# Products x @ w_ch made in earlier chunks, two of them kept in the places of results, in an attention and spectral-mixing kernel

## Chip, cores, metric

One core of a Trainium2 chip. The metric is the time of the whole program on the device in microseconds, the median of several runs.

## The reference, cut to what matters

```python
x = attention(q, k, v, s)                    # 8 batches, 8 heads, 576 positions, 64 wide -> [8, 576, 512]
X = rfft(x, axis=1)[:, :64]                  # 64 modes
Y = X @ (w_r + i w_i)                        # one 512 x 512 complex matrix per mode: 134 MB of fp32 weights
y = irfft(Y, n=576)
u = x + y
out = u + max(u @ w_ch, 0)
```

By linearity u @ w_ch = x @ w_ch + y @ w_ch, so the part x @ w_ch, here called a *product*, can be made for each pair of 128-row blocks (18 pairs) before y is known.

## The kernel before

The mode weights come in 128 tiles of 512 KB (they are bf16 on the chip, half the size of the fp32 in memory) through one transfer queue and are used in four groups of eight *chunks*, four tiles a chunk. The last group's chunks run after the attention; between them TensorE makes products of *late* pairs, whose results are kept on chip. The product of a pair is 8 matmuls of 128x512, after 8 small ones that transpose x.

```python
    NLOC = 4
    places = [finpool.tile([P, 4 * DM], BF16, name=f"z1_{i}") for i in range(NLOC)]
    places.append(old[:, 4 * DM : 8 * DM])
    places += [y_acc[:, c : c + 2, :]... for c in (0, 2)]
    # later products: a buffer of the weight ring
    ...
    late = [i for i in kept if i not in first_pairs]
    TAKE = (2, 2, 1, 2, 0, 3)                # products in chunks 0 to 5 (one is made a step later)
    ...
    for c in range(NCK - 2):                 # chunks 0 to 5
        yb = modes(NG - 1, c)
        for x in range(TAKE[c] - 1):
            work()                           # transposes one late pair; makes the product of the one before
        yt = y_transposed(yb)
        if TAKE[c]:
            work()
        y_times_wch(c, yt)                   # v = y @ w_ch of this chunk
    work()
    c = NCK - 2                              # chunk 6
    for i in range(NPRE):                    # pairs 0 and 1 are not kept: their products stay in PSUM
        x_transposed(i)
    yb = modes(NG - 1, c)
    yt = y_transposed(yb)
    y_times_wch(c, yt)
    for i in range(NPRE):
        x_times_wch(i, False)
    start_u(0)                               # u 0 = x + ...
    add_y(us[0], 0, 0, slice(0, GK))         # ... + y of chunks 0 to 6; waits for the spread of y
    def first_sums():
        for i in range(NPRE):
            add_y(z_of(i), i, 1, slice(0, GK))   # waits for the spread of v
    yb = modes(NG - 1, NCK - 1, first_sums)  # chunk 7: three groups, first_sums, the last group
    # from here on, the tail: y and v of chunk 7, then sums, ReLU and output of 18 pairs
```

y and v of each chunk are *spread* by a transfer of 128 KB from one on-chip tile to another before the sums can use them.

The softmax here doesn't subtract the row's maximum and nothing guards it: scores larger than these inputs give would overflow.

## Time and profile before

| | before |
|---|---|
| time, median of 3 | 463.88 us (462.47 to 464.22) |
| span of the profiled execution | 462.2 us |
| TensorE busy, VectorE, ScalarE | 75%, 51%, 47% of the span |
| last weight tile lands | 421.6 us |
| last group of chunk 7 starts | 423.75 us |
| from there to the end | 38.45 us |

The span runs from the first to the last instruction of one profiled execution; the times are some 1.8 us above it. No engine's share says what bounds this kernel: one must look at the point where the weights end. The prediction shows those lines.

### The profile page before, as it was taken

Reading aid. Unit: us, or ns where it says so; the run is one execution under the profiler, and the core shown is the slowest. Engines: PE = TensorE matmul, PEld = TensorE weight load, DVE = VectorE, ACT = ScalarE, POOL = GpSimd, SP = SyncE. Lnnn points to the kernel's source line nnn. Section 1 sums busy time; section 2 is a strip of 40 time slices with the busy share of each in tenths; the row PEclk is TensorE's granted clock in tenths of the full one; section 3 lists DMA queues with packets and bytes.
Section 4 is the critical chain, followed back from the end, with each engine's and each line's share of the span. In section 5 each row is a group of like instructions: output and inputs, shape, how many; then the busy total and the mean of one; then the engine's idle time right before and its main releaser. Section 6 shows DMA issues by size and latency. Waiting matters only on the chain.

```text
span 462.2 us, 10263 instructions
## 1 busy us (share of the span) xinstructions
PE 345.9 (75%) x4185; PEld 215.8 (47%) x4185; DVE 233.6 (51%) x523; ACT 219.1 (47%) x382; POOL 182.9 (40%) x269
## 2 busy tenths in 40 slices
PE   1879968977663989647397586798976767578996
PEld 1556646755441666434265354565642423244442
DVE  7676654753332657524265335557553432171676
ACT  1677865564342667624265434556610202031895
POOL 6655544544444455344454444455232222100000
PEclk9998996995776899958789859899997767599999
DMA  9999999999999999999999999999999999992697
GB/s 179 201 202 203 202 200 203 203 204 204 204 204 198 204 202 203 204 204 205 199 194 205 204 204 205 205 202 202 206 211 213 215 212 214 214 210 59 223 307 302
DMA packets 110063, 95.16 MB, mean 206 GB/s; under 512 B 28544, under 2 KB 105216, under 8 KB 110016
## 3 DMA queue, kind: packets, MB, share of 16 engines
q0 software_dynamic: 98960, 81.81, 111.7%
q1 hardware_dynamic: 11056, 12.70, 8.9%
q8 instruction: 33, 0.54, 0.4%
q14 instruction: 14, 0.11, 0.1%
HBM read 164.66 MB, written 9.44 MB: 377 GB/s over the span
## 4 chain that ended last, share of the span: by engine, by line
DMA 66%; PE 22%; issue 4%; DVE 4%; POOL 3%; ACT 0%; DVEq 0%; POOLq 0%; ACTq 0%
DMA w_sb<-in_moe_w_i_dram 40%; DMA w_sb<-in_moe_w_r_dram 8%; DMA q<-in_q_dram 7%; DMA k<-in_k_dram 5%; PE yp L441 3%; PE av_ps L394 2%; PE sc_ps L365 2%; DMA x_all<-in_moe_w_r_dram 2%; PE z_ps L598 2%; DMA y_acc<-in_moe_w_r_dram 2%; PE z_ps L657 2%; DMA y_acc<-in_moe_w_i_dram 2%; PE u_ps L676 2%; PE tr_ps L324 2%; PE u_ps L657 2%
## 5 line engine op out<-in xcount | busy, mean ns | idle before, releaser
L373 ACT ACTIVATE p_sb<-sc_ps,cumt_sb 128x576 f16<-128x576 f32 (+1 forms) x256 | 141.8, 635 | 48.1 <-PE sc_ps L365 47.6
L217 POOL DMA_DIRECT2D w_sb<-in_moe_w_i_dram x60 | 45.0, 751 | 80.8 <-DMA w_sb<-in_moe_w_i_dram 34.1
L217 POOL DMA_DIRECT2D w_sb<-in_moe_w_r_dram x60 | 45.3, 756 | 69.4 <-DMA w_sb<-in_moe_w_r_dram 24.0
L217 POOL DMA_DIRECT2D v<-in_v_dram x72 | 50.7, 707 | 31.7 <-DMA v<-in_v_dram 9.5
L441 PE MATMUL yp<-w_sb,xs 128*32 128x512 bf16 x480 | 38.9, 424 | 24.9 <-DMA w_sb<-in_moe_w_i_dram 20.9
L324 PE MATMUL tr_ps<-ident,q 64*64 64x64 bf16 x576 | 17.2, 209 | 52.4 <-DMA q<-in_q_dram 52.4
L359 PE MATMUL sc_ps<-negm,ident 128*128 128x256 bf16 x256 | 56.0, 305 | 0.2
L327 DVE COPY qtA<-tr_ps 64x576 bf16<-64x576 bf16 x32 | 23.8, 743 | 46.8 <-PE tr_ps L324 46.8
L394 PE MATMUL av_ps<-v,p_sb 128*128 128x65 f16 x1024 | 45.8, 200 | 0.0
L344 ACT ACTIVATE p<-sc_ps,cumt 128x64 f16<-128x64 f32 x32 | 10.0, 313 | 72.0 <-PE sc_ps L340 72.0
L394 PEld LDWEIGHTS <-p_sb 128*128 128x128 f16 x1024 | 40.7, 102 | 5.1 <-issue 1.0
L365 PE MATMUL sc_ps<-qtB,ktB 128*128 128x512 bf16 (+2 forms) x192 | 42.3, 336 | 0.0
L327 DVE COPY ktA<-tr_ps 64x576 bf16<-64x576 bf16 x32 | 24.0, 749 | 33.3 <-PE tr_ps L324 33.2
L441 PEld LDWEIGHTS <-xs 128*32 128x32 bf16 x512 | 22.7, 169 | 36.3 <-issue 32.9
L324 PEld LDWEIGHTS <-q 64*64 64x64 bf16 x576 | 13.4, 121 | 55.2 <-DMA q<-in_q_dram 54.4
L365 PE MATMUL sc_ps<-qtA,ktA 65*128 65x512 bf16 (+2 forms) x192 | 38.2, 310 | 0.5 <-DMA qtA<-ncum_sb 0.5
L399 DVE TENSOR_REDUCE den<-av_ps 128x5 f32<-128x10 f32 x64 | 10.8, 169 | 51.1 <-PE av_ps L394 51.1
L404 DVE TENSOR_TENSOR x_all<-av_ps,rcp 128x320 f16<-128x320 f32 x64 | 31.4, 491 | 2.2
L327 ACT COPY ktB<-tr_ps 64x576 bf16<-64x576 bf16 x32 | 20.3, 633 | 21.4 <-DVE ktA L327 20.4
L324 PE MATMUL tr_ps<-ident,k 64*64 64x64 bf16 x576 | 17.2, 208 | 16.2 <-DVE qtB L327 10.3
L365 PEld LDWEIGHTS <-ktB 128*128 128x128 bf16 x192 | 21.8, 114 | 14.0 <-issue 5.2
L598 PE MATMUL z_ps<-wch_sb,xs 128*128 128x512 f16 x96 | 28.1, 448 | 0.0
(103 smaller groups left out, 516.4 us busy)
## 6 DMA issues: line engine op xcount, KB each, us to landing
w_sb<-in_moe_w_r_dram POOLq DMA_DIRECT2D x60, 512.0 KB, 11.9
w_sb<-in_moe_w_i_dram POOLq DMA_DIRECT2D x60, 512.0 KB, 11.9
q<-in_q_dram POOLq DMA_DIRECT2D x32, 144.0 KB, 9.8
k<-in_k_dram POOLq DMA_DIRECT2D x32, 144.0 KB, 10.1
v<-in_v_dram POOLq DMA_DIRECT2D x72, 64.0 KB, 9.7
out_dram<-r_sb SPq DMA_DIRECT2D x16, 256.0 KB, 2.1
out_dram<-r_w SPq DMA_DIRECT2D x16, 256.0 KB, 2.6
x_all<-in_moe_w_i_dram POOLq DMA_DIRECT2D x3, 512.0 KB, 9.8
```

The costliest lines, as they stand in the source:

```text
L217: nc.gpsimd.dma_start(out=dst, in_=src)
L324: nc.tensor.transpose(ps[rows, r, :], src[rows, r, :], ident16[rows, rows])
L327: copy(out=dst[n % NQ][rows, :].rearrange("d (p r) -> d p r", r=R), in_=ps[rows].rearrange("d r p -> d p r"),)
L359: nc.tensor.matmul(ps[:, bass.ds(w * S, W)], ident16, negm[:, bass.ts(r, W)], start=True, stop=False, skip_group_check=True,)
L365: nc.tensor.matmul(ps[:, c0 : c0 + i1 - i0], keys[:, w, r, :], qt[:, i0:i1], start=False, stop=True, skip_group_check=True,)
L373: nc.scalar.activation(out=pt[:, poff[x] : poff[x] + S - w * W], in_=ps[:, w * S : (w + 1) * S - w * W], func=ACTF.Exp, bias=cumt_sb[:, x, ...
L394: nc.tensor.matmul(ps[:, I, r : r + NCH], lhsT, rhs, start=(i == 0), stop=(i == len(todo) - 1), skip_group_check=True,)
L399: nc.vector.tensor_reduce(out=den, in_=ps[:, :, 0 : VW : NCH], axis=mybir.AxisListType.X, op=ALU.add)
L404: nc.vector.tensor_tensor(out=x_all[:, g, b, :, D * h : D * h + D], in0=ps[:, :, 1 : NCH], in1=rcp.unsqueeze(2).to_broadcast([P, NT, D]), ...
L441: nc.tensor.matmul(ps[32 * cg : 32 * cg + 32, :], cols[:, c0 : c0 + 32, c * MC + 2 * cg + par], wt[(g, c, ri, par)][:, cg, :], start=(x == ...
L598: nc.tensor.matmul(z[:, x, :], xts[i][:, x, dt, :], wch_sb[:, dt, :], start=(dt == 0), stop=(last and dt == DT - 1), skip_group_check=True,)
L657: nc.tensor.matmul(dst[x][r, :], G_sb[rows, bass.ds(T * P, r.stop - r.start)], yv[rows, bb, which, :], start=start, stop=True, skip_group_ ...
```

## The change

Its intent is to have no product left over when the last weights arrive. It finds three more places for kept products (two are the places where results 2 and 4 will be written, which needs pairs 2 and 4 to be the first late ones, so pair 9 takes pair 2's turn in the attention loop), moves the late products to chunks 0 to 4 (the last of them, made one step later, falls between chunks 5 and 6), and makes pair 0's product ahead of chunk 6.

```diff
-    first_pairs = [i for i in kept if pairs[i][0][1] < NF and pairs[i][0][0] <= 3]
+    first_pairs = [i for i in kept[1:] if pairs[i][0][1] < NF and pairs[i][0][0] <= 4][:6]
...
-    NLOC = 4
+    NLOC = 5
...
-    places = [finpool.tile([P, 4 * DM], BF16, name=f"z1_{i}") for i in range(NLOC)]
+    places = [finpool.tile([P, 4 * DM], BF16, name="r_sb", tag="r", bufs=3) for i in range(2)]
+    places += [finpool.tile([P, 4 * DM], BF16, name=f"z1_{i}") for i in range(NLOC)]
...
-    TAKE = (2, 2, 1, 2, 0, 3)
+    TAKE = (3, 2, 2, 2, 1, 0)
...
+    x_times_wch(0, False)
     yb = modes(NG - 1, c)
     yt = y_transposed(yb)
     y_times_wch(c, yt)
-    for i in range(NPRE):
-        x_times_wch(i, False)
+    x_times_wch(1, False)
```

(The results' tile is also declared in another type, of the same size.)

## The prediction

> **What bounds the kernel now.** I read the page first, then the chain of waits in order of time, then TensorE's timeline near its end. The page's row of DMA shares says that the transfers are full for 36 of 40 slices, and the row of bytes says what ends there:
>
> ```profile
> DMA  9999999999999999999999999999999999992697
> GB/s 179 201 202 203 202 200 203 203 204 204 204 204 198 204 202 203 204 204 205 199 194 205 204 204 205 205 202 202 206 211 213 215 212 214 214 210 59 223 307 302
> ```
>
> A slice is 462.2 / 40 = 11.56 us, so the weights stop streaming in slice 37, between 416 and 428 us. After that only results go out. The chain of waits (start, duration, what) shows when the chain leaves the weights:
>
> ```profile
> 354.03 22.74 DMA w_sb<-in_moe_w_i_dram
> ...
> 377.30 21.94 DMA w_sb<-in_moe_w_i_dram
> ...
> 399.28 0.67 PE yp L441 x3
> 399.95 0.97 PE xt_ps L588 x8
> 400.92 2.44 PE z_ps L598 x8
> ```
>
> Up to 399.28 us each step waits for a weight tile. The last such tile is the fourth of chunk 5 (counting from 0); from there to the end the chain is TensorE, VectorE and ScalarE work. The eight tiles of chunks 6 and 7 are still under way at 399.28. TensorE's timeline (start, duration, line, output, and in brackets the idle time before) shows that it comes too late to both chunks and waits for neither:
>
> ```profile
> 399.28 0.67 PE L441 MATMUL yp<-w_sb,xs 128*32 128x512 bf16 x4 [2.25 <-DMA w_sb<-in_moe_w_i_dram]
> ...
> 413.52 1.12 PE L441 MATMUL yp<-w_sb,xs 128*32 128x512 bf16 x16
> ...
> 421.94 0.91 PE L441 MATMUL yp<-w_sb,xs 128*32 128x512 bf16 x12
> 422.78 1.04 PE L657 MATMUL z_ps<-yv,G_sb 112*128 112x512 f16 x4
> 423.75 0.47 PE L441 MATMUL yp<-w_sb,xs 128*32 128x512 bf16 x4
> ```
>
> When did those tiles land? The list of transfers, asked for the last issue alone (it begins at 399.77 us), gives the time from issue to landing:
>
> ```profile
> w_sb<-in_moe_w_i_dram POOLq DMA_DIRECT2D x1, 512.0 KB, 21.8
> ```
>
> So the last tile lands at 399.77 + 21.8 = 421.6. In the same way the issue at 388.30 with 21.5 us gives 409.8 for the last tile of chunk 6, and those at 391.40, 394.46 and 396.84 with 21.0, 20.5 and 21.2 give 412.4, 415.0 and 418.0 for the first three of chunk 7. TensorE thus takes chunk 6 at 413.52, 3.7 us after it is complete, and the last group of chunk 7 at 423.75, **2.15 us after its tile landed**. What follows, from 423.75 to 462.2, is a tail of 38.45 us on which TensorE is 9.88 and 10.00 us busy in the stretches 430:440 and 440:450.
>
> [...] Stretches of 3.41 us laid on the trace's own changes of clock (length, busy TensorE us, ..., granted clock, DMA share, GB/s):
>
> ```profile
> 361.26:364.68 3.42, 1.38 (x18) 0.73 (x16) 1.18 (x2) 0.54 (x1) 0.74 (x1) 1.00 1.24 206
> 371.50:374.92 3.42, 1.68 (x15) 0.67 (x14) 1.82 (x2) 0.38 (x1) 0.90 (x2) 1.00 1.24 206
> 337.37:340.78 3.41, 2.20 (x26) 1.29 (x24) 1.66 (x5) 0.58 (x1) 2.15 (x4) 1.00 1.24 206
> 412.46:415.88 3.42, 2.22 (x28) 1.33 (x27) 2.58 (x5) 0.20 (x1) 0.00 (x0) 1.00 1.19 205
> ```
>
> The first two, 40% and 49% busy, are each followed by half clock; the last two, 64% and 65%, are not. I take about half busy as the limit, an estimate from these lines. The same product of eight 128x512 matmuls takes 1.89 us at full clock and 3.62 us at half clock in this trace. [...] a 128 KB spread of y or v takes 7.4 us to land beside the weights (issued 400.72) and 3.3 us when they run out (418.37). [...] work that follows the weights is put into the idle time between weight tiles.
>
> **The change part by part.** *Places.* Ten late pairs are kept before and after. Before, seven have places of their own and three must wait for weight buffers, so chunk 4 gives no product and chunk 5 three. Now two lie where results will be written, one more tile is added, and no weight buffer is used. Result 2 takes the place of pair 2's product and result 4 that of pair 4's; each is written by the ReLU that reads a sum for which that product was already read. I see no new wait, so 0.
>
> *Pair 9 for pair 2 in the attention loop.* Both are kept in the two-part form, so the six early pairs still have two such and four others. The counts do not change and the loop waits for weights: 0.
>
> *Products to earlier chunks.* Before, chunk 5 and the step after it do three transposes of pairs and four products after 399.28; after, one product. Three products and three transposes leave: the products cost 2.64 + 1.89 + 1.89 = 6.4 us, the transposes 1.03 + 0.61 + 0.76 = 2.4 us, and with 0.77 us of waits for VectorE's copies that is 9.6 us of TensorE time. They land in chunks 0, 2 and 4. There TensorE waits for tiles: 2.46 and 1.91 us in chunk 1, 1.56 and 2.07 in chunk 3, 2.35 and 2.25 in chunk 5. Chunk 4 ends at 388.27; with one product more (4.6 us at half clock with its transpose) TensorE is ready for chunk 5 near 396, and the last tile of that lands at 399.2. So 0 here, and no transfer starts late: eight tiles are on the queue, some 21 us of work.
>
> *Pair 0's product ahead of chunk 6, pair 1's after it.* No work is added. From 399.95 the order is: y of chunk 5, its transposes and v (to about 403.2, half of it at half clock), one product (404.9), four transposes with their copies (407.0), product 0 (408.8), chunk 6 (its last tile is there at 409.8; done 410.3), y and v of it (413.2), product 1 (414.9), start of u 0 (415.4). Then TensorE waits for y's spread (issued 411.0, about 6 us: 417), chunk 7's third tile (418.0), v's spread (413.9 + 6 = 420), and last for the tile at **421.6** instead of starting at 423.75. So of some 9.6 us taken out only 2.15 us can come off the end; the rest turns into waiting for weights. Sum with a warm TensorE: 463.9 - 2.1 = 461.8.
>
> *The clock.* Between 414.9 and 421.6 TensorE now has about 3.0 us of work in 6.7 us (start 0.5, sums 0.5, three groups 0.8, first sums 1.0, and the wait edges), under one half. A 3.41 us window that lies there will most likely be under the limit, and half clock is then granted just as the tail begins. It lasts one or two windows; of these 3.4 to 6.8 us fall into the tail, where about three quarters of the time is TensorE's (3.1 of 4.1 us from 423.75 to 427.84). The loss is 0.5 x 0.75 x (3.4 to 6.8) = 1.3 to 2.5 us, about 1.9. Chance some 0.7, as the windows' phase is not the kernel's. Expected: 463.9 - 2.15 + 0.7 x 1.9 = 463.0; with a little for what I count too darkly, **462.8 us**.
>
> **The rivals.** *A, the whole wait goes and the clock stays up:* 461.8. For it: first sums and groups are spread over the gap, and 53% busy might suffice. Against it: windows of 40% and 49% busy throttled. *B, the waiting takes the clock down and nothing is gained:* 463.5 to 464. For it: the lines above. Against it: only part of the tail's head is TensorE work. *C, TensorE's backlog was the true bound and all of the 9.6 us comes off:* 454.3. For it: the chain after 399.28 contains no weight transfer. Against it: the landing at 421.6, which the change does not move, as the bytes are the same. *D, a product kept in a result's place or the fuller chunk 4 makes a wait of its own:* 465 to 466. For it: a third of the places moved. Against it: TensorE has 3 us of room before chunk 5's last tile.
>
> **Range and chances.** A and B span 461.8 to 464; the three runs of before span 1.75 us (462.47 to 464.22). I widen each side by about 1 us: 460.8 to 464.8. To be faster by over 2% the time must be under 454.6, which only C gives: 0.03. Slower by over 2% is over 473.2, beyond D: 0.01. Within 2%: 0.96.
>
> **What would show it.** In the profile after: chunk 6's groups should no longer come in one block of 16 but wait for a tile near 409.8; the last group should start near 421.7 with idle time before it that a weight transfer ends; the last landing should stay within 1 us of 421.6; the tail should last 38.5 us at full clock, about 40 us if half clock is granted between 418 and 428. I am wrong if the last weight lands earlier or later by over 1 us, if chunk 5's last group starts after 400, or if the tail's length changes at full clock.

Its sum: 463.9 - 2.15 + 0.7 x 1.9 = 463.1 us (it says 463.0), and from there it goes to 462.8. The limit of about half busy is the author's estimate from the four stretches, and the chance of 0.7 is an estimate whose size has no working.

What it assumes of the clock can be read from the traces. In those of before and after the granted clock is 0.5 or 1 and nothing between, and each whole interval between two changes is a multiple of 3.41 us: 3.4 to 17.1 us at half clock and 3.4 to 61.4 us at full clock. Near the end half clock then lasted two such windows in the kernel after (419.97 to 426.80, 6.8 us) and one in e9b (419.05 to 422.46, 3.4 us). The windows lie at other places in another execution of the same kernel: one begins at 416.38 in e9a and at 415.64 in e9b.

## The result, and the profile after

464.03 us (463.36 to 465.47, 6 runs) against 463.76 us (462.47 to 464.28, 6 runs): a ratio of 1.0012, with a 95% interval of 0.9993 to 1.0032. The ratio here and below is the mean time of one kernel's fast runs over that of the other's of the same rounds, so not quite the ratio of the medians. Nothing was gained.

Yet the profile shows that the change moved the work as it meant to. TensorE's timeline of the kernel after, where chunk 5 ends, then from chunk 6 on (start, duration, line, operation, idle time before):

```profile
397.95 0.67 PE L441 MATMUL yp<-w_sb,xs 128*32 128x512 bf16 x4 [2.04 <-DMA w_sb<-in_moe_w_i_dram]
...
402.44 3.62 PE L600 MATMUL z_ps<-wch_sb,xs 128*128 128x512 f16 x8
...
408.07 1.89 PE L600 MATMUL z_ps<-wch_sb,xs 128*128 128x512 f16 x8
409.89 1.12 PE L441 MATMUL yp<-w_sb,xs 128*32 128x512 bf16 x16
...
413.81 1.89 PE L600 MATMUL z_ps<-wch_sb,xs 128*128 128x512 f16 x8
415.54 0.59 PE L678 MATMUL u_ps<-x_all,ident16h 128*128 128x512 f16 x2
418.11 0.61 PE L659 MATMUL u_ps<-yv,G_sb 112*128 112x512 f16 x2 [1.97 <-DMA yv<-y_sb]
418.64 0.91 PE L441 MATMUL yp<-w_sb,xs 128*32 128x512 bf16 x12
420.46 1.87 PE L659 MATMUL z_ps<-yv,G_sb 112*128 112x512 f16 x4 [0.92 <-issue]
422.26 0.68 PE L441 MATMUL yp<-w_sb,xs 128*32 128x512 bf16 x4
...
424.84 1.92 PE L762 MATMUL v_ps<-wch_sb,yt_sb 128*128 128x256 f16 x8
```

Chunk 6 starts 3.6 us earlier than before (409.89 against 413.52). One late product (402.44) is left between chunks 5 and 6, where there were four; behind it stands pair 0's (408.07), which used to come after chunk 6. From 416 us on TensorE waits, 1.97 us for y's spread and 0.92 us ahead of the first sums. For the second wait the trace names no releaser, but the sums read v's spread, which was issued at 414.73 with 5.6 us to landing, so it was there at 420.3, just before they start. Then the same instructions take longer: the four matmuls of the first sums 1.87 us instead of 1.04, the last group 0.68 instead of 0.47, v of chunk 7 1.92 instead of 1.04 (its line before stands here; those of the sums and of the last group stand in the prediction):

```profile
425.63 1.04 PE L758 MATMUL v_ps<-wch_sb,yt_sb 128*128 128x256 f16 x8
```

That is the half clock. The page's row of granted clock, before and then after, has it in one digit, slice 37 (416 to 428 us), 9 before and 7 after:

```profile
PEclk9998996995776899958789859899997767599999
```

```profile
PEclk9997999997777979958789978899998889697999
```

Stretches of 3.41 us in the kernel after, laid on the trace's changes of clock (span, length, TensorE busy us, weight loads, VectorE, ScalarE, GpSimd, **granted clock**, DMA share, GB/s), show when it fell:

```profile
413.14:416.56 3.42, 3.00 (x14) 1.18 (x12) 0.69 (x1) 0.00 (x0) 0.00 (x0) 1.00 1.22 218
416.56:419.97 3.41, 1.44 (x14) 0.56 (x14) 0.00 (x0) 0.00 (x0) 0.00 (x0) 1.00 0.70 131
419.97:423.38 3.41, 2.48 (x8) 0.61 (x8) 0.39 (x2) 0.00 (x0) 0.00 (x0) 0.50 0.00 0
423.38:426.80 3.42, 3.33 (x16) 2.02 (x17) 0.80 (x4) 0.65 (x2) 0.00 (x0) 0.50 0.16 43
```

The stretch with the two waits is 1.44 / 3.41 = 42% busy; the next two, from 419.97 to 426.80, run at half clock. This is the moment when the last tile lands (issued 398.44, 22.1 us to landing: 420.5) and the tail begins.

Where the time went, from the two profiled executions: the last group starts 1.49 us earlier (422.26 against 423.75). From it to the start of TensorE's last two matmuls it takes 34.68 us (to 456.94) against 33.25 (to 457.00): 1.43 us lost. TensorE is thus done only 0.06 us earlier. From there to the end is 5.76 us against 5.20, in VectorE's last sums and the output transfers, whose median from issue to landing is 2.7 us there against 2.1; that 0.56 us I count as a difference of single executions. The sum, -1.49 + 1.43 + 0.56 = +0.50 us, is the difference of the spans (462.7 and 462.2).

Not all of what was missed is the clock's. With its tile there at 420.5 the last group could have started 3.25 us earlier than before; it started 1.49 us earlier. Of the missing 1.76 us, 0.83 us is the half clock in the first sums (1.80 us from their start to the group's, 0.97 before). The other 0.93 us is v's spread: with sums that start at 420.46 the group could not have started before 421.4 even at full clock. So in this one execution, by an estimate from these lines, the half clock cost 0.83 + 1.43 = 2.3 us and the spread 0.9 us.

### The profile page after: what moved, and what is told of

It reads as the page before. It is cut to its first block, busy times and chain, and to the rows that moved or that the text cites. A ratio compares the mean times of both kernels' runs of the same rounds, so it can differ in the third digit from the quotient of the medians.

```text
span 462.7 us, 10254 instructions
## 1 busy us (share of the span) xinstructions
PE 344.4 (74%) x4185; PEld 215.3 (47%) x4185; DVE 233.6 (50%) x523; ACT 219.5 (47%) x382; POOL 182.9 (40%) x269
## 4 chain that ended last, share of the span: by engine, by line
DMA 63%; PE 24%; DVE 5%; issue 4%; POOL 2%; ACT 0%; SPq 0%; DVEq 0%; POOLq 0%; ACTq 0%
DMA w_sb<-in_moe_w_i_dram 24%; DMA w_sb<-in_moe_w_r_dram 17%; DMA q<-in_q_dram 15%; PE sc_ps L365 4%; PE av_ps L394 3%; PE sc_ps L359 3%; DMA k<-in_k_dram 2%; PE tr_ps L324 2%; PE z_ps L659 2%; PE u_ps L659 2%; PE u_ps L678 2%; PE yp L441 2%; POOL w_sb L217 1%; DMA yv<-y_sb 1%; PE z_ps L784 1%
## 5 line engine op out<-in xcount | busy, mean ns | idle before, releaser
L441 PE MATMUL yp<-w_sb,xs 128*32 128x512 bf16 x480 | 37.3, 409 | 23.3 <-DMA w_sb<-in_moe_w_i_dram 18.8
L394 PE MATMUL av_ps<-v,p_sb 128*128 128x65 f16 x1024 | 44.8, 198 | 0.0
L365 PE MATMUL sc_ps<-qtB,ktB 128*128 128x512 bf16 (+2 forms) x192 | 43.9, 346 | 0.0
L365 PE MATMUL sc_ps<-qtA,ktA 65*128 65x512 bf16 (+2 forms) x192 | 37.0, 302 | 0.4 <-DMA qtA<-ncum_sb 0.4
```

The costliest lines, as they stand in the source:

```text
L365: nc.tensor.matmul(ps[:, c0 : c0 + i1 - i0], keys[:, w, r, :], qt[:, i0:i1], start=False, stop=True, skip_group_check=True,)
L394: nc.tensor.matmul(ps[:, I, r : r + NCH], lhsT, rhs, start=(i == 0), stop=(i == len(todo) - 1), skip_group_check=True,)
L441: nc.tensor.matmul(ps[32 * cg : 32 * cg + 32, :], cols[:, c0 : c0 + 32, c * MC + 2 * cg + par], wt[(g, c, ri, par)][:, cg, :], start=(x == ...
```

## Experiments

Theory, *clock*: the idle time that the change makes just ahead of the tail drops TensorE to half clock (42% busy from 416.56 to 419.97, a clock of 0.50 after it), and what that costs in the first sums and the tail's head cancels the gain. Rivals: *places*, results that share places with kept products wait, so the tail is longer for that; *spreads*, the last group now waits for v's spread whatever TensorE's clock, so the bound only changed its name; *order*, pair 0's early product delays y and v of chunk 6.

| run | what | median us (runs) | ratio to before, 95% interval | last tile lands | last group starts |
|---|---|---|---|---|---|
| before | | 463.76 (6) | | 421.6 | 423.75 |
| after | the change | 464.03 (6) | 1.0012 (0.9993 to 1.0032) | 420.5 | 422.26 |
| e1_filler | after, 13 unread matmuls in the waits | 460.91 (6) | 0.9947 (0.9926 to 0.9967) | 420.4 | 420.69 |
| e8_filler_first | after, the first 8 of them | 461.40 (6) | 0.9946 (0.9928 to 0.9964) | 420.3 | 420.96 |
| e5_filler_before | before, 13 unread matmuls | 466.33 (6) | 1.0050 (1.0036 to 1.0063) | 421.8 | 427.13 |
| e3_places_only | before, new places and pair swap | 464.23 (6) | 1.0010 (0.9992 to 1.0028) | 421.2 | 425.23 |
| e4_z0_only | before, pair 0's product early | 464.11 (6) | 1.0016 (0.9997 to 1.0035) | 419.8 | 423.59 |
| e2_z0_back | after, pair 0's product late | 463.20 (6) | 0.9985 (0.9970 to 1.0001) | 420.6 | 421.93 |
| e6_spread_work | after, own work put between the waits | 463.49 (6) | 0.9985 (0.9969 to 1.0002) | 420.5 | 421.61 |
| e9a, e9b | e6 again, one execution each | 461.58 and 463.67 | | 420.4, 420.8 | 420.97, 423.06 |
| e7_one_in_c5 | after, one product back in chunk 5, pair 0's late | 461.41 (6) | 0.9947 (0.9934 to 0.9960) | 420.6 | 420.72 |
| e10_one_in_c5_z0_early | after, one product back in chunk 5 | 462.24 (5) | 0.9974 (0.9961 to 0.9988) | 419.9 | 421.39 |

The landing is the last issue's start plus its time to landing, from each run's own list of transfers. Landings and starts are those of the one profiled execution. The kernel before had medians of 463.66 us in the rounds of e1 to e4, 463.96 in those of e5 to e8 and 463.78 in those of e10. The results of all experiments were correct.

### Filler in the idle time (e1_filler, e8_filler_first)

```diff
     start_u(0)
+    fill_ps = auxpool.tile([P, DM], FP32, name="fill_ps", tag="aux")
+    def filler(n):
+        for _ in range(n):
+            nc.tensor.matmul(fill_ps, ident16h, wch_sb[:, 0, :], start=True, stop=True, skip_group_check=True)
+    filler(8)
     add_y(us[0], 0, 0, slice(0, GK))
     def first_sums():
+        filler(5)                            # not in e8_filler_first
         for i in range(NPRE):
```

> The changed kernel with 13 matmuls of 128x512 added whose result nobody reads: 8 after the start of u 0 and 5 ahead of the first sums, where TensorE waits for the spreads of y and v of chunk 6. Clock theory (idle time drops the clock to half just as the tail begins, which costs 2.0 us): the clock stays full from 406 us on, the tail from the last group of chunk 7 to the end is 38.5 us and not 40.4, and the time is 461.7 to 462.5, some 2 us under the kernel before. Rival, the tail is longer because results and kept products share places: the tail stays near 40.4 us and the time at 464 or above, since work was only added. Rival, the landing of v's spread is the new bound: the last group starts at the same 422.3 with filler or without, and the time is near 464.

> The changed kernel with the first 8 unread matmuls alone. Clock theory: the gap before y's spread is filled and the one before the last group is not (some 1.3 us idle), so a window stays near half busy; the clock holds in most runs, 460.8 to 462.5, with more spread between runs than with both. If the gap just ahead of the tail is the one that matters: 463 to 464.

With 13 matmuls more the kernel is 0.5% faster than before (460.91 us). TensorE's timeline of the run with both fillers:

```profile
415.27 1.89 PE L746 MATMUL fill_ps<-wch_sb,ident16h 128*128 128x512 f16 x8
417.05 0.61 PE L659 MATMUL u_ps<-yv,G_sb 112*128 112x512 f16 x2
417.59 0.91 PE L441 MATMUL yp<-w_sb,xs 128*32 128x512 bf16 x12
418.43 1.25 PE L746 MATMUL fill_ps<-wch_sb,ident16h 128*128 128x512 f16 x5
419.74 1.02 PE L659 MATMUL z_ps<-yv,G_sb 112*128 112x512 f16 x4
420.69 0.47 PE L441 MATMUL yp<-w_sb,xs 128*32 128x512 bf16 x4
...
422.58 1.04 PE L772 MATMUL v_ps<-wch_sb,yt_sb 128*128 128x256 f16 x8
```

Sums, last group and v are back at 1.02, 0.47 and 1.04 us. The last group starts 0.3 us after its tile landed, and from there to the last matmuls (453.77) it takes 33.08 us (33.25 before). The places are the same as in the changed kernel, so they don't explain its loss. v's spread takes the same 5.6 us, so it doesn't explain the slower matmuls either; what the filler changed is TensorE's busy share (3.41 of 3.41 us from 415.11 to 418.52 and 2.82 of 3.41 us from 418.52 to 421.93) and with it the clock, 1.00 in both stretches and in the next. But the spread keeps a part: in this execution the half clock in the late product ended sooner (3.08 us against 3.62), before any filler ran, and v's spread was issued 0.70 us earlier. Of the 1.57 us by which the last group comes earlier than in the changed kernel, 0.72 us is the earlier start of the sums and 0.85 us their full clock.

The first eight alone do as well (461.40, the same ratio), with 2.8 us between the fastest and the slowest run (460.38 to 463.20). So it is not the gap just ahead of the last group that has to be filled.

### The same filler in the kernel before (e5_filler_before)

The same edit, in the kernel before.

> The kernel before with the same 13 unread matmuls in the same two places. There TensorE comes late to every tile of chunks 6 and 7 and its clock is full, so the clock theory gives the filler nothing to save: its 13 x 0.216 = 2.8 us go onto the end, 466.3 to 466.9. If the filler helps in some other way (the wait that it shifts, the buffer that it takes), this is under 464 too.

Here it costs nearly what it takes (2.8 us for 13 matmuls of 0.216 us; in the trace before, eight of this size took 1.73 us from their start to the next instruction's, 403.63 to 405.36): 466.33 us, 2.4 us over before, with the last group at 427.13. From 404.29 on its matmuls up to the tail take the times of full clock: eight of a product or of the filler 1.89 us, the first sums 1.03, v of chunk 7 1.04. So filler had no use of its own here. It paid only where TensorE otherwise idled (e1, 2.75 us under before in the same rounds).

### Parts of the change alone (e3_places_only, e4_z0_only, e2_z0_back)

`e3_places_only` is the change with both of these undone, `e2_z0_back` with the second undone; `e4_z0_only` is the kernel before with the second done.

```diff
-    TAKE = (3, 2, 2, 2, 1, 0)
+    TAKE = (2, 2, 1, 2, 0, 3)               # e3 only
...
-    x_times_wch(0, False)                   # ahead of chunk 6
     yb = modes(NG - 1, c)
     yt = y_transposed(yb)
     y_times_wch(c, yt)
-    x_times_wch(1, False)
+    for i in range(NPRE):
+        x_times_wch(i, False)
```

> The kernel before with the new places and pair 9 for pair 2 alone; the products stay in their old chunks and pair 0's product behind chunk 6. Clock theory: the same backlog as before, TensorE busy up to the tail, nothing gained or lost: 463.4 to 464.2. If results that share places with kept products add a wait: 465 or above, with a tail over 38.5 us.

> The kernel before with pair 0's product ahead of chunk 6 alone. TensorE's backlog is as large, only its order differs: y and v of chunk 6 come 1.75 us later, the last group no earlier. Clock theory: 463.4 to 464.5, full clock in the tail. If the order itself brings a loss (the spreads of chunk 6 land later and hold up the sums): 464.5 to 466.

> The changed kernel with the product of pair 0 put back behind chunk 6 (the places and the earlier products stay). Clock theory: 1.75 us of work moves into the gap between 414 and 418, TensorE is over half busy there, keeps full clock, and still arrives before the last tile lands: 461.7 to 462.8. If the move of pair 0's product is what helps in the change: slower than the changed kernel, 464.5 to 466. If the places make the tail longer: 464 as the changed kernel.

The places and the swap cost nothing that can be told from noise (464.23 us; the tail is 38.4 us), which agrees with the filler run against the rival. Pair 0's early product alone changes nothing either (464.11). As long as the late products stand between chunks 5 and 6 (four, and pair 0's with them in e4), TensorE's backlog sets the end: the last group starts 4.0 and 3.8 us after its tile.

`e2_z0_back` missed the expectation: 463.20 us, not 461.7 to 462.8. Its stretches (columns as above) say why. The gap had not gone, it had moved ahead of chunk 6, whose last tile TensorE now waits for:

```profile
407.22:410.63 3.41, 0.99 (x16) 0.41 (x8) 0.87 (x2) 0.00 (x0) 0.00 (x0) 1.00 1.22 217
410.63:414.04 3.41, 2.34 (x9) 0.98 (x10) 0.28 (x1) 0.59 (x1) 0.00 (x0) 0.50 1.24 206
414.04:417.46 3.42, 3.42 (x10) 1.21 (x9) 0.69 (x1) 0.00 (x0) 0.00 (x0) 0.50 1.15 213
```

29% busy, then half clock for 6.8 us; the two products after chunk 6 take 5.34 us instead of 3.62, and the last group comes 1.3 us after its tile. So this run does not refute the clock theory but my picture of where the idle time lies.

### The changed kernel's own work between the waits (e6_spread_work, e9a, e9b)

```diff
...                                          # x_times_wch takes the halves to make as an argument
-    x_times_wch(1, False)
+    x_times_wch(1, False, (0,))             # first half of pair 1's product
-    start_u(0)
-    add_y(us[0], 0, 0, slice(0, GK))
     def first_sums():                       # behind the third group of chunk 7
+        x_times_wch(1, False, (1,))         # second half
+        start_u(0)
+        add_y(us[0], 0, 0, slice(0, GK))
         for i in range(NPRE):
```

> The changed kernel without filler, its own work in another order: half of pair 1's product, the start of u 0 and its sums come behind the first three groups of chunk 7. Clock theory: the idle time is cut into pieces of under 1.7 us between real work, the clock mostly stays full, 460.8 to 462.3. If what helps in the filler run is only the added work and not where TensorE idles: 464 as the changed kernel. Rival of late sums: u 0's sums now come behind the third tile, the last group starts 1 us later, 462.5 to 463.5.

The median, 463.49 us, missed; yet the profiled execution, with full clock, was the fastest (462.06). The median lies in the range of the rival of late sums, and this rival holds in part: even at full clock the sums started at 420.65, as v's spread landed (issued 414.66, 5.9 us: 420.6), and the last group at 421.61, 1.1 us after its tile. To see what parts the slow runs from the fast ones, the kernel was run twice more for its trace.

> The kernel of the run with spread work once more, for a second trace: its six times were 462.06 to 464.59 and the one profiled, with full clock in the tail and one stretch of exactly half busy, was the fastest. Clock theory: where the time is over 463, half clock is granted in a stretch that reaches into the tail, and the tail is over 39.5 us; where it is near 462, it is not. Rival: the slower ones have a later last landing or a longer tail at full clock.

> As the run before it, a third trace of the same kernel, same expectation: time and tail go with the clock granted between 416 and 427 us.

The two executions differ by 2.1 us, 461.58 and 463.67. These are single runs; the traces show the difference. First e9a, then e9b (columns as above):

```profile
412.97:416.38 3.41, 2.14 (x16) 0.90 (x14) 0.69 (x1) 0.00 (x0) 0.00 (x0) 1.00 1.21 220
416.38:419.80 3.42, 2.00 (x12) 0.86 (x11) 0.00 (x0) 0.00 (x0) 0.00 (x0) 1.00 0.64 111
419.80:423.21 3.41, 2.83 (x20) 1.16 (x19) 0.75 (x2) 0.65 (x2) 0.00 (x0) 1.00 0.01 1
```

```profile
412.22:415.64 3.42, 2.73 (x16) 1.11 (x17) 0.69 (x1) 0.29 (x1) 0.00 (x0) 1.00 1.23 211
415.64:419.05 3.41, 0.75 (x6) 0.36 (x6) 0.00 (x0) 0.00 (x0) 0.00 (x0) 1.00 0.83 147
419.05:422.46 3.41, 3.41 (x10) 1.22 (x8) 0.00 (x0) 0.00 (x0) 0.00 (x0) 0.50 0.06 13
```

The program is the same, and the wait for the third tile of chunk 7 is nearly the same, 2.69 us in one and 3.00 in the other, starting just after 415 in both. In e9a the boundary of two stretches, 416.38, cuts the wait, and both parts stay over half busy (63% and 59%). In e9b the boundary, 415.64, leaves nearly the whole wait in one stretch, 22% busy, and half clock follows. The last group starts 0.6 us after its tile in e9a and 2.3 us after it in e9b. Some 0.5 us of the 2.1 us is not the clock's: the third tile came later in e9b (the wait ends at 418.30, in e9a at 417.80). From there to the last group it takes 4.76 us against 3.17, and these 1.6 us are the half clock. I had expected the loss in the tail (over 39.5 us); it came ahead of the last group instead, and the tail was 38.8 us in both. With two traces this is shown for two executions; that the six timed ones divide in the same way is likely, not shown.

### Work left where TensorE needs it (e7_one_in_c5, e10_one_in_c5_z0_early)

```diff
-    TAKE = (3, 2, 2, 2, 1, 0)
+    TAKE = (3, 2, 2, 2, 0, 1)
...                                          # e7 only: both first pairs' products behind chunk 6, as in e2
```

> The changed kernel with one product moved back to chunk 5 (none in chunk 4) and both first pairs' products behind chunk 6. Clock theory: TensorE has work from chunk 5 until chunk 6 is complete and from there until about 419, so it neither throttles nor arrives over 1 us late: 460.8 to 462.3. If all ten products must be early to gain: 463 or more.

> The changed kernel with one product moved back to chunk 5, but with pair 0's product still ahead of chunk 6. Clock theory: chunk 6 comes about 1 us late (near 411), y's spread lands near 419, and TensorE idles some 2 us before it, so in part of the runs the clock falls: 462 to 463.5, wider between runs than with both products behind chunk 6. If only the number of early products matters: 461.4 as that run. If pair 0's early product is the whole harm: 463.5 or more.

With one product given back to chunk 5 and pair 0's given back to its old place, 461.41 us, 0.5% under before, with real work alone and only 0.8 us between the fastest and the slowest run. TensorE's timeline of that run:

```profile
405.22 1.89 PE L600 MATMUL z_ps<-wch_sb,xs 128*128 128x512 f16 x8
...
409.03 1.12 PE L441 MATMUL yp<-w_sb,xs 128*32 128x512 bf16 x16
...
412.95 3.62 PE L600 MATMUL z_ps<-wch_sb,xs 128*128 128x512 f16 x16
...
417.57 0.90 PE L441 MATMUL yp<-w_sb,xs 128*32 128x512 bf16 x12
419.77 1.02 PE L659 MATMUL z_ps<-yv,G_sb 112*128 112x512 f16 x4 [1.29 <-issue]
420.72 0.47 PE L441 MATMUL yp<-w_sb,xs 128*32 128x512 bf16 x4
```

The work reaches up to chunk 6's last tile without a gap, both products then run at full clock, and one gap of 1.29 us is left. The stretch with it is 2.13 / 3.42 = 62% busy. The last group starts 0.1 us after its tile. The same with pair 0's product early is 462.24 us: chunk 6 comes at 411.16, y's spread later, and a gap of 1.64 us stands before it. In its one trace the stretches round that gap are 54% and 55% busy and the clock stays full, so there the 0.8 us is lateness and not clock (the last group starts 1.5 us after its tile). Both kernels are faster than the change; e7 is the best version with no wasted work, and e1 with filler is its equal.

## Why the prediction was right, point by point

- *The end is set by the last tile plus the tail, and only some 2 us of the 9.6 us taken out can come off.* Right in size. With the clock held up (e1, e7) the gain is 0.53%, 2.5 us, near the 2.15 us of the prediction and far from the 9.6 us of its rival C. The rest of the gain may come from landings near 420.5 instead of 421.6; four traces with the old backlog give 421.6, 421.2, 421.8 and 419.8, the others 419.9 to 420.8. Whether early products bring the last tile in earlier stays open. The order of the last waits was not as predicted, though: the tile, to be waited for until 421.6, was there at 420.5, and the sums that need v's spread (420.3) ended after it. In the profiled execution, and in those of e6 and e8, it is these sums that the last group comes behind.
- *The clock falls as the tail begins and takes the gain back.* The mechanism is right, and rival B (463.5 to 464) is what was measured. The term that was mis-sized is the chance, "some 0.7": none of the six runs came near 461.8, the fastest was 463.36; that the clock fell in all six is likely, but only one was traced. A second mis-sizing is where the cost falls: only the part in the tail was counted, 1.3 to 2.5 us; it measured 1.43 us there, and 0.83 us more (1.87 against 1.04) in the first sums, ahead of the last group. Both together bring the predicted 461.8 of a warm TensorE to 464.06, next to the measured 464.03; that the earlier tile and the later sums nearly cancel is luck. So the estimate of 462.8 was 1.2 us too low, inside its range.
- *Chunk 6's groups wait for a tile near 409.8.* Wrong: they came in a block of 16 at 409.89. The late product (402.44) still ran at half clock, 3.62 us where 1.7 was reckoned, and so used up the wait.
- *Places and the swap, 0.* Right (e3, 464.23 us against 463.66 in the same rounds, within noise). *More products in chunks 0 to 4, 0.* Right: chunk 5's last group started at 397.95.
- *The last landing within 1 us of 421.6, the tail about 40 us.* The tail is right, 40.44 us. The landing is not: at 420.5 it is 1.1 us earlier, so one of the prediction's own signs of being wrong was met.
- *Slips in the working, none of which turns it.* From 423.75 to 427.84 the trace before has TensorE 3.38 of 4.09 us busy, not 3.1 of 4.1. Rival A's 53% has no working and doesn't fit the text's own 3.0 of 6.7 us, 45% (42% was measured). At 399.28 the eighth tile was not yet under way (issued 399.77). The sum given as 463.0 is 463.1.

## What to carry to other kernels

Where TensorE waits for weights and a TensorE-bound tail follows, being early to the last tile was not free here: a stretch only 42% busy just ahead of the tail (1.44 of 3.41 us) was followed by half clock for 6.8 us, the first sums and the tail's head. Take out of the backlog only as much as makes TensorE arrive on time, and leave the rest of the work to fill the waits (e7, 461.41 us), or fill them with matmuls nobody reads (e1). When a change removes a wait and the time stays, look at the same instructions' durations before and after: here the sums went from 1.04 to 1.87 us.

How much idle time is too much? Of the stretches of 3.41 us at full clock in the traces of before and after (from 20 us on), those followed by half clock were 49% busy or less, and those of 52% or more kept full clock. The limit is not sharp: one stretch of 46% (kernel after, 385.84 to 389.25, 1.56 of 3.41 us) kept it too, and so did one of 50% in e6 (416.50 to 419.92, 1.69 of 3.42 us). One of 65% followed by half clock was noted in e5 (263.12 to 266.53, 2.20 of 3.41 us), but no answer kept from its trace shows it. So the busy share in the profile is a sign and not the rule. Short gaps were enough: 1.97 and 0.92 us with work between them (kernel after, 42% busy). With a single gap near 3 us it depended on where the boundary fell: 3.00 us in e9b lay nearly whole in one stretch, 22% busy, and half clock followed; 2.69 us in e9a was cut in two stretches of 63% and 59%, and it did not.

Ask also how long a small transfer takes beside the weights. From 384 us on in the kernel after, the spreads of 128 KB took 5.6 to 6.3 us from issue to landing while weights came in, and 2.9 to 3.1 us when those were gone. The wait for y's spread is one of the two in which TensorE idled.
